# A fused attention and token-mixing MLP kernel: uneven filler batches, one paired maximum per stretch, and bursts cut in two in the MLP1 stage

## The chip, the cores and the metric

The kernel runs on one core of a Trainium2 chip. The metric is the device time of one execution in microseconds (us), the median of several runs. The time of a run is slightly longer than the span of its profile, which goes from the first to the last instruction.

## What is computed

```python
x = A_x                                             # (1, 2048, 640)
g = sigmoid((x * gate_w).sum(-1, keepdims=True))
# a: attention, 32 query heads of 20, one shared key/value head
q = (x @ wq).reshape(B, S, H, Dh).transpose(0, 2, 1, 3)
scores = einsum("bhqd,bkd->bhqk", q, x @ wk) * (Dh ** -0.5)
o = einsum("bhqk,bkd->bhqd", softmax(scores, axis=-1), x @ wv)
a = o.transpose(0, 2, 1, 3).reshape(B, S, H * Dh) @ wo
# b: MLP over the token axis
h = layernorm(x)                                    # (B, S, D)
u = gelu(einsum("bsd,sf->bdf", h, w1) + b1)         # F = 1728
b = (einsum("bdf,fs->bds", u, w2) + b2).transpose(0, 2, 1)
return g * a + (1 - g) * b
```

S is 2048, D is 640, F is 1728. The softmax subtracts a row maximum, so every score is computed twice: once as a "max tile" (queries on the partitions, reduced over 512 keys by VectorE) and once as a "score tile" (keys on the partitions, 512 queries, to which ScalarE applies the exponential).

## The kernel before

**Stages.** A prologue (projections, layer norm, the first ten tiles of the first MLP product) ends near 186 us. Then 248 **stretches** follow, counted by `j` in the loop `for j in range(n_st)`. Each holds 8 score tiles (`qk`, L689), some max tiles (`ms_next`, L507), some **fillers** (matmuls of 320 columns of the MLP or of the output projection), and ends in a **burst** (`burst`, L725): the products of exponentials and values for two key blocks, four heads side by side on the columns of the array. Stretches 0 to 71 take their fillers from the first MLP product (`b1_jobs`, L1020): this is the **MLP1 stage**. The next 128 take them from the second product (`b2_jobs`, L845), the last 48 from the output projection (`a_jobs`, L973).

**Two lanes.** Score tiles, max tiles and fillers contract over at most 64 rows, so two of them run at a time, one on each row half of the array. In stretch `j` the lane `h = j % 2` is the **own lane**: it holds the 8 score tiles and `own` max tiles. The **filler lane** holds the fillers and the remaining max tiles. A burst uses the whole array, so it begins only behind the last tile of both lanes.

**MLP1 before.** One tile of the first product is 96 steps, 48 for each lane. `batches` cuts them into two batches of 24, and each batch makes two stretches, one for each lane. A stretch holds 10 max tiles: `share` gives 8 to the own lane and 2 to the filler lane. The filler lane runs one max tile, 24 fillers and one max tile; the own lane runs `ssmSSmmssmssmmmm`, where `SS` is a pair of score tiles in neighbouring banks that one exponential of 1024 columns reads.

**Banks.** Seven PSUM banks rotate among score tiles, max tiles and the burst's sum (`xs3` has 3 neighbouring banks, `xs4` has 4); an eighth accumulates the fillers. A bank is taken again when ScalarE or VectorE has read it. The evicting copy of a burst (L749) is in ScalarE's queue, its addition to the running sum (L752) in GpSimd's.

**What sets the order.** A planner (`begins`, `issue`, `arrange`) keeps estimated clocks for the lanes, the banks, VectorE and ScalarE, and at each step issues the tile that can begin first. `begins` lets a filler start when its lane is free, and a tile that needs a bank only when its estimate says that one is free. The outcome is one fixed list of instructions for each engine. On the chip, semaphores decide when an instruction begins, but its place in the list is fixed.

**Weights.** The first product's weights arrive in chunks of 12 steps (`w1_upto`): GpSimd casts a chunk (L126) and subtracts (L127) for its low part. In this stage four chunk buffers serve, one of which is lent to queries, and the place of each conversion follows from the first and last use of its chunk.

Of the kernel before, what the change touches and what calls it, by code (L numbers as in the profile page):

```python
# [19 lines left out]
S, D, H, DH, F = 2048, 640, 32, 20, 1728  # L20
# [5 lines left out]
NB = 512  # L26
# [13 lines left out]
def mix_kernel(ctx: ExitStack, tc: tile.TileContext, A_x, A_wq, A_wk, A_wv, A_wo,  # L40
               B_x, B_w1, B_b1, B_w2, B_b2, gate_w, out):
    nc = tc.nc
    x = A_x[0]
# [440 lines left out]
    def span(i, n):  # L484
        t, at = (xs[0], i) if i < 3 else (xs[1], i - 3)
        return t[:, at * NB:(at + n) * NB]

    row_max, stores = {}, []
    mtiles = {}
# [3 lines left out]
    def ms_next(b):  # L493
        k = given[b]
        if k >= 32 * NU or k // 32 not in qtiles:
            return None
        given[b] += 1
        n, r = divmod(k, 32)
        (kq, pr), qt = divmod(r // 4, 2), r % 4

        def step(i=None):
            if n not in mtiles:
                mtiles[n] = mpool.tile([P, 16, 4], F32, name="mp")
            if i is None:
                turns[0] += 1
            ms = pre[turns[0] % 4].tile([P, NB], F32, name="x" if turns[0] % 4 else "g") if i is None else bank(i)
            mm = nc.tensor.matmul(ms, qtiles[n][64 * b:64 * b + 60, pr, qt * P:(qt + 1) * P],  # L507
                                  kst[64 * b:64 * b + 60, kq * NB:(kq + 1) * NB], start=True, stop=True)
            region = [("x", i)] if i is not None else []
            if region:  # L510
                touch(mm, writes=region)
            out = mtiles[n][:, (2 * b + pr) * 4 + qt, kq:kq + 1]

            def reduce():
                red = nc.vector.tensor_reduce(out, ms, axis=AX.X, op=ALU.max)  # L515
                if region:
                    touch(red, reads=region)
                issued[b] += 1

            return reduce  # L520

        return step

    def ms_done():
# [501 lines left out]
        return load, [([[of_chunk(base + st // HS, lambda h=h, st=st, k=k: mm(st, k, h)) for h in range(2)]  # L1026
                        for st in range(NS) for k in range(3)], done)]

    def batches(tiles, counts):
        out = []  # L1030
        for n, (load, parts, *_) in enumerate(tiles):
            for d, (steps, done) in enumerate(parts):
                cnt = counts.pop(0)
                rows = [[f[h] for f in steps if len(f) > h] for h in range(2)]
                cut = [[len(r) * j // cnt for j in range(cnt + 1)] for r in rows]
                for j in range(cnt):
                    rest = []
                    if d == 0 and j == 0 and n + 1 < len(tiles):
                        rest.append(tiles[n + 1][0])
                    out.append(([r[c[j]:c[j + 1]] for r, c in zip(rows, cut)], rest, [done] if j == cnt - 1 else []))  # L1040
        return out

    n_st = (len(units) - TAIL) // 2
    todo = [divmod(i, FC) for i in range(PRO, 2 * FC)]
    seq = batches([b1_jobs(*t) for t in todo], [2] * len(todo))
    m = len(seq)
    seq += batches([b2_jobs(st) for st in range(NS)], [2] * 2 * NS)
    seq[-1][1].append(second)
# [17 lines left out]
    step = 0  # L1066
# [13 lines left out]
    X_US, F_US, O_US = 0.2345, 0.1468, 0.869  # L1080
    W_US, FIRST_US, LAST_US, NEXT_US, SEEN_US = 0.11, 0.1, 0.333, 0.13, 0.43
    EACH = {"dve": (0.6, 0.84), "act": (0.48, 0.815)}
    PAIR_US = 0.85
    clock = {"dve": 0.0, "act": 0.0}
    lane, fresh, free = [0.0, 0.0], [True, True], [0.0] * 3 + [1.3] * 4
    state = {"at": 0.0, "f": 0.0, "last": 0.0}
# [2 lines left out]
    def spend(e, us, at=0.0):  # L1089
        clock[e] = max(clock[e], at) + us  # L1090
        return clock[e]
# [8 lines left out]

    def begins(h, kind):
        at = max(lane[h] + W_US * fresh[h], state["at"])
        if kind == "S":
            return max(at, pair[1] if pair else free[next_pair()])
        return max(at, state["f"] if kind in "fe" else min(free))

    def issue(h, kind, f):
        at = state["at"] = begins(h, kind)
        fresh[h] = False
        lane[h] = at + (F_US if kind in "fae" else X_US)  # L1110
        state["last"] = at
        if kind in "fae":
            f()
        elif kind == "S":
            if not pair:
                i = next_pair()
                pair[:] = [i, free[i + 1]]
                free[i] = free[i + 1] = float("inf")
            else:
                i = pair[0] + 1  # L1120
                begin = spend("act", PAIR_US, at + SEEN_US) - PAIR_US
                free[i - 1] = free[i] = begin + PAIR_US + EACH["act"][1] - EACH["act"][0]
                pair.clear()
            while any(k == i for _, k, _ in reduces):
                reduces.pop(0)[2]()
            f(i)
        else:
            i = next_free()
            each, hold = EACH["act" if kind == "s" else "dve"]
            begin = spend("act" if kind == "s" else "dve", each, at + SEEN_US) - each  # L1130
            free[i] = begin + hold
            while any(k == i for _, k, _ in reduces):
                reduces.pop(0)[2]()
            g = f(i)
            if kind == "m":
                reduces.append((begin, i, g))

    pairs = {}

    def layout(n_s, n_m, n_f, n_o):  # L1140
        if n_f > 22 and n_o > 1:
            places = [0, n_f]
        elif n_f > 22:
            places = [0]
        elif n_s + n_m < 13:
            places = [0, n_f - 4]
        else:
            places = [0, n_f]
        places = (places + [n_f // 2, 3 * n_f // 4])[:n_o]
        lf = ""  # L1150
        for i in range(n_f + 1):
            lf += "m" * places.count(i) + "f" * (i < n_f)
        lf += "m" * (n_o - lf.count("m"))
        if n_f > 22 and (n_s, n_m, n_o) == (8, 8, 2):
            return "ssmSSmmssmssmmmm", lf
        lx = "sSS" if n_s + n_m > 12 else "s"
        s, m = n_s - len(lx), n_m
        a, b = s, m
        while s or m:
            if m and (not s or m * a >= s * b):  # L1160
                lx, m = lx + "m", m - 1
            else:
                lx, s = lx + "s", s - 1
        return lx, lf

    def arrange(h, ss, own, other, fs, end):
        ss, own, other, fs = list(ss), list(own), list(other), list(fs)
        n_s, n_m, n_f = len(ss), len(own), len(fs)
        lx, lf = layout(n_s, n_m, n_f, len(other))
        pairs.clear()  # L1170
        at = lx.replace("m", "").find("S")
        if at >= 0:
            pairs.update({at: 0, at + 1: 2})
        lx = [(k, (own if k == "m" else ss).pop(0)) for k in lx]
        lf = [(k, (other if k == "m" else fs).pop(0)) for k in lf]
        lanes = [None, None]
        lanes[h], lanes[1 - h] = lx, lf
# [66 lines left out]
    def share(j):  # L1244
        h, to = j % 2, owed + wants[j]
        own = round((min(to, 9) + F_US / X_US * len(ph[j][0]) - 8) / 2)
        if h:
            own = (given[0] - given[1] + to + 1) // 2
        own = min(to, max(0, own))
        return (to - own, own) if h else (own, to - own)  # L1250

    for j in range(n_st):
# [36 lines left out]
        if j == 8 * 25 - 1:  # L1289
            new_q(29)  # L1290
        if j:
            burst((2 * j - 2, 2 * j - 1), (0, NB // 2, NB) if 15 < len(ph[j][0]) <= 22 else (0, NB))
        if j == n_st - 2:
            raw = last_wo()

# [185 lines left out]
```

## Time and profile before

| | before |
|---|---|
| median of 3 runs | 1597.38 us (1596.97 to 1598.45) |
| the profiled execution | 1597.11 us |
| its span | 1595.3 us |
| busy: PE, VectorE, ScalarE, GpSimd | 100%, 86%, 81%, 53% of the span |
| granted TensorE clock | 0.999 |
| MLP1 stretches | from 186.8 us (first burst) to 610.8 us (last) |

Instructions are named by line and operand tiles: L507 is a max tile's matmul, L515 its reduction, L689 a score tile, L701 its exponential, L1020 a filler of the MLP1 stage, L725 a burst. PE busy is a modelled share: matmuls overlap, so 100% says only that some matmul was always under way. What a stretch costs is read from the starts of the bursts, and from the pace at which each lane's matmuls begin.

### The profile page before, as it was taken

The page shows a single profiled execution, that of the slowest core. Times are in us where ns is not written, and L with a number is a line of the kernel's source. Part 1 is how long each engine was busy: PE and PEld are TensorE (multiplying, and loading weights), DVE is VectorE, ACT ScalarE, POOL GpSimd, SP SyncE. Part 2 cuts the span into 40 slices and gives each one's busy share as a digit, 9 for nine tenths or more (in the row PEclk, how much of TensorE's full clock was granted, in tenths as well). Part 3 has the DMA queues.
Part 4 walks back from the last instruction along what each step waited for, and adds up shares of the span by engine and source line. Part 5 has one row for each costly group of instructions (what it writes and reads, how often), then busy time and mean ns, then how long its engine had stood idle before and what let it go on. Part 6 is the DMA issues. An engine that isn't in the chain of part 4 may idle for free.

```text
span 1595.3 us, 43453 instructions
## 1 busy us (share of the span) xinstructions
PE 1589.4 (100%) x16907; PEld 1184.3 (74%) x16907; DVE 1379.2 (86%) x2626; ACT 1295.4 (81%) x2481; POOL 845.0 (53%) x930
## 2 busy tenths in 40 slices
PE   9999999999999999999999999999999999999998
PEld 7899876767677677777777777777777776666665
DVE  6689999999999999999999999999999996667743
ACT  4445677778787788888888888888888889999996
POOL 6567767777777777545554344444444433333340
PEclk9999999999999999999999999999999999999999
DMA  7665323222222232322121122122221113322341
GB/s 218 204 172 141 95 61 71 66 75 73 73 69 68 57 76 55 91 70 70 49 63 55 48 62 58 55 61 62 62 61 48 49 41 107 113 84 83 90 137 59
DMA packets 180452, 129.78 MB, mean 81 GB/s; under 512 B 41617, under 2 KB 150062, under 8 KB 180246
## 3 DMA queue, kind: packets, MB, share of 16 engines
q1 hardware_dynamic: 179958, 126.68, 28.6%
q8 instruction: 133, 2.18, 0.6%
q14 instruction: 73, 0.60, 0.1%
q10 hardware_dynamic: 288, 0.33, 0.1%
HBM read 93.57 MB, written 32.15 MB: 79 GB/s over the span
## 4 chain that ended last, share of the span: by engine, by line
PE 98%; SPq 1%; DVE 0%; ACT 0%; DMA 0%; issue 0%; DVEq 0%
PE xs L725 30%; PE xs L689 18%; PE xs L507 18%; PE g L845 11%; PE g L1020 7%; PE pu L634 4%; PE pp L303 4%; PE g L973 3%; PE x L507 1%; PE xs L927 1%; PE pt L295 0%; SPq L200 0%; DVE st L236 0%; PE xs L1426 0%; PE g L927 0%; PE xs L1446 0%
## 5 line engine op out<-in xcount | busy, mean ns | idle before, releaser
L515 DVE TENSOR_REDUCE mp<-xs 128x1 f32<-128x512 f32 x1946 | 1197.1, 682 | 133.0 <-PE xs L689 79.3
L701 ACT ACTIVATE p<-xs 128x512 f32<-128x512 f32 (+1 forms) x1841 | 1016.2, 677 | 7.4 <-PE xs L689 3.4
L752 POOL TENSOR_TENSOR osum<-osum,part 128x512 f32<-128x512 f32 x216 | 279.4, 1294 | 596.8 <-ACT part L749 574.8
L725 PE MATMUL xs<-p,v_sb 128*32 128x256 f32 (+1 forms) x6144 | 493.6, 454 | 0.0
L689 PE MATMUL xs<-q,kst 62*128 62x512 f32 x1344 | 476.9, 418 | 0.0
L507 PE MATMUL xs<-kst,q 60*128 60x512 f32 x1242 | 426.6, 407 | 0.0
L725 PEld LDWEIGHTS xs<-p,v_sb 128*32 128x32 f32 x6144 | 173.6, 109 | 210.7 <-issue 81.4
L689 PEld LDWEIGHTS xs<-q,kst 62*128 62x128 f32 x1344 | 236.8, 185 | 56.7 <-DVE mp L515 22.6
L749 ACT ACTIVATE part<-xs 128x256 f32<-128x256 f32 (+1 forms) x328 | 148.8, 454 | 157.1 <-PE xs L725 155.7
L1020 PE MATMUL g<-slot,w 64*128 64x320 f32 x1728 | 266.2, 305 | 0.0
L1020 PEld LDWEIGHTS g<-slot,w 64*128 64x128 f32 x1728 | 259.0, 184 | 1.8
L507 PEld LDWEIGHTS xs<-kst,q 60*128 60x128 f32 x1242 | 212.0, 184 | 50.3 <-DVE mp L515 19.3
L127 POOL TENSOR_TENSOR w<-wr,w 128x512 fp32r<-128x512 f32 (+1 forms) x180 | 225.0, 1252 | 35.1 <-ACT w L124 22.6
L689 PE MATMUL xs<-slot,kst 62*128 62x512 f32 x569 | 207.5, 418 | 0.0
L845 PE MATMUL g<-u,w 64*128 64x320 f32 x1296 | 200.4, 305 | 0.0
L845 PE MATMUL g<-slot,w 64*128 64x320 f32 x1296 | 200.4, 305 | 0.0
L507 PE MATMUL xs<-kst,slot 60*128 60x512 f32 x576 | 200.3, 408 | 0.0
L845 PEld LDWEIGHTS g<-u,w 64*128 64x128 f32 x1296 | 195.2, 184 | 1.6
L845 PEld LDWEIGHTS g<-slot,w 64*128 64x128 f32 x1296 | 195.2, 184 | 1.6
L973 PE MATMUL g<-slot 64*128 64x320 f32 x720 | 118.2, 306 | 0.0
L689 PEld LDWEIGHTS xs<-slot,kst 62*128 62x128 f32 x569 | 100.3, 185 | 20.1 <-ACT part L749 7.4
L973 PEld LDWEIGHTS g<-slot 64*128 64x128 f32 x720 | 111.8, 185 | 4.3 <-DVE mm L537 0.8
(190 smaller groups left out, 1435.7 us busy)
## 6 DMA issues: line engine op xcount, KB each, us to landing
wr<-in_B_w_dram SPq DMA_DIRECT2D x155, 256.0 KB
q<-q_scr SPq DMA_DIRECT2D x126, 80.0 KB
rb<-r_scr SPq DMA_DIRECT2D x120, 64.0 KB
slot<-o_scr SPq DMA_DIRECT2D x24, 320.0 KB
y_scr<-yo SPq DMA_DIRECT2D x16, 320.0 KB
q_scr<-qh SPq DMA_DIRECT2D x19, 256.0 KB
q_scr<-ql SPq DMA_DIRECT2D x19, 256.0 KB
o_scr<-rb SPq DMA_DIRECT2D x120, 40.0 KB
```

The costliest lines, as they stand in the source:

```text
L127: nc.gpsimd.tensor_sub(wl, wr, f32(wh))
L303: nc.tensor.matmul(pp, w, t, start=first and n == 0, stop=not more and n == len(steps) - 1)
L507: mm = nc.tensor.matmul(ms, qtiles[n][64 * b:64 * b + 60, pr, qt * P:(qt + 1) * P], kst[64 * b:64 * b + 60, kq * NB:(kq + 1) * NB], start= ...
L515: red = nc.vector.tensor_reduce(out, ms, axis=AX.X, op=ALU.max)
L689: mm = nc.tensor.matmul(s, kst[64 * b:64 * b + 62, kb * P:(kb + 1) * P], q[64 * b:64 * b + 62, pr, :], start=True, stop=True)
L701: act = nc.scalar.activation(p_all[:, a * NB:(j + 1) * NB], s, AF.Exp, scale=SCALE)
L725: mm = nc.tensor.matmul(o[32 * hh:32 * hh + 32, at:to], v_sb[:, units[u][1], :], p_all[:, j * NB + at:j * NB + to], start=first, stop=last ...
L749: touch(nc.scalar.activation(t[:, at:to], o[:, at:to], AF.Copy), [("x", i)])
L752: nc.gpsimd.tensor_add(osum[n], osum[n], t)
L845: other_tile(half, nc.tensor.matmul(hold["p"][:, :HD2], w[r, fc % HS, :], u[d][r, fc, :], start=(hold["n"] == 1), stop=(hold["n"] == 6 * F ...
L973: other_tile(half, nc.tensor.matmul(hold["p"][:, :HD2], o[r, c, :], w[r, c, d * HD2:(d + 1) * HD2], start=(hold["n"] == 1), stop=(hold["n" ...
L1020: other_tile(half, nc.tensor.matmul(hold["p"][:, :HD2], w[r, st % HS, :], h[d][r, st, :], start=(hold["n"] == 1), stop=(hold["n"] == 6 * NS)))
```

## The change

Four things change, all of them in the MLP1 stage:

- `batches` gets `more=1` there: the 48 steps of a lane are cut into 25 and 23. Two stretches of 25 and two of 23 alternate.
- A stretch of 25 has 9 max tiles in its own lane and 1 in the filler lane; a stretch of 23 has 8 and 2, as before. There are still 10.
- Two of the own lane's max tiles form a pair `M`, in neighbouring banks, and one reduction of 1024 columns gives both maxima. The own lane's order is a new string. Where two maxima would not lie side by side in the result tile (`turns`), the pair changes places with a single max tile. The paired exponential `SS` is gone from this stage.
- `burst` is cut into two halves of the queries, each with its own bank and its own eviction, as it already is in the stretches with 20 or 21 fillers.

```diff
...
-        def step(i=None):
+        def step(i=None, part=0):
...
-            out = mtiles[n][:, (2 * b + pr) * 4 + qt, kq:kq + 1]
+            col = (2 * b + pr) * 4 + qt
+            if part == 1:
+                return None
+            both = part == 2
+            out = mtiles[n][:, col - both:col + 1, kq]
+            if both:
+                ms = span(i - 1, 2).rearrange("p (a k) -> p a k", a=2)
+                region.append(("x", i - 1))
...
-                issued[b] += 1
+                issued[b] += 1 + both
...
+        step.turns = r % 8 == 7
...
-    def batches(tiles, counts):
+    def batches(tiles, counts, more=0):
...
-                cut = [[len(r) * j // cnt for j in range(cnt + 1)] for r in rows]
+                cut = [[len(r) * j // cnt + more * (0 < j < cnt) for j in range(cnt + 1)] for r in rows]
...
-    seq = batches([b1_jobs(*t) for t in todo], [2] * len(todo))
+    seq = batches([b1_jobs(*t) for t in todo], [2] * len(todo), 1)
...
-    PAIR_US = 0.85
+    PAIR_US = {"act": 0.85, "dve": 1.13}
...
-        if kind == "S":
+        if kind in "SM":
...
-        elif kind == "S":
+        elif kind in "SM":
+            e = "act" if kind == "S" else "dve"
...
-                begin = spend("act", PAIR_US, at + SEEN_US) - PAIR_US
-                free[i - 1] = free[i] = begin + PAIR_US + EACH["act"][1] - EACH["act"][0]
-                pair.clear()
+                begin = spend(e, PAIR_US[e], at + SEEN_US) - PAIR_US[e]
+                free[i - 1] = free[i] = begin + PAIR_US[e] + EACH[e][1] - EACH[e][0]
+                pair.append(begin)
...
-            f(i)
+            if kind == "S":
+                f(i)
+            else:
+                g = f(i, len(pair) - 1)
+                if g:
+                    reduces.extend(((begin, i - 1, g), (begin, i, lambda: None)))
+            if len(pair) > 2:
+                pair.clear()
...
-    def layout(n_s, n_m, n_f, n_o):
+    def layout(n_s, own, n_f, n_o):
+        n_m = len(own)
...
-        if n_f > 22 and (n_s, n_m, n_o) == (8, 8, 2):
-            return "ssmSSmmssmssmmmm", lf
+        if n_f > 22 and (n_s, n_m, n_o) == (8, 10 - n_o, n_o):
+            lx = list("smssmssmsmsmsMmm" if n_o == 1 else "smsmsssmmssmmsM")
+            at = lx.index("M")
+            if own[lx[:at].count("m")].turns:
+                to = at + 1 if "m" in lx[at:] else max(i for i in range(at) if lx[i] == "m")
+                lx[at], lx[to] = lx[to], lx[at]
+            return "".join(lx).replace("M", "MM"), lf
...
-        n_s, n_m, n_f = len(ss), len(own), len(fs)
-        lx, lf = layout(n_s, n_m, n_f, len(other))
+        n_f = len(fs)
+        lx, lf = layout(len(ss), own, n_f, len(other))
...
-        at = lx.replace("m", "").find("S")
+        at = lx.replace("m", "").replace("M", "").find("S")
...
-        lx = [(k, (own if k == "m" else ss).pop(0)) for k in lx]
+        lx = [(k, (own if k in "mM" else ss).pop(0)) for k in lx]
...
+        if len(ph[j][0]) > 22 and to == 10:
+            own = 8 + (len(ph[j][0]) > 24)
...
-            burst((2 * j - 2, 2 * j - 1), (0, NB // 2, NB) if 15 < len(ph[j][0]) <= 22 else (0, NB))
+            burst((2 * j - 2, 2 * j - 1), (0, NB // 2, NB) if len(ph[j][0]) > 15 else (0, NB))
...
```

Program order is shown below at three places. `xs_2756` is the tile of 3 banks, `xs_2760` that of 4; `g` is the fillers' bank; `kst` are keys, `q` and `slot_79` queries, `p` exponentials, `w_90` and `w_92` weight chunks. L507, L515, L689, L725 and L1020 are L507, L522, L697, L733 and L1028 in the changed kernel.

TensorE before, the end of the stretch whose burst is the 29th of the program; the last row is that burst:

```order
L1020 MATMUL g<-slot_80,w_90 128x320
L689 MATMUL xs_2760<-q,kst 128x512
L1020 MATMUL g<-slot_80,w_90 128x320 x2
L507 MATMUL xs_2760<-kst,slot_79 128x512
L1020 MATMUL g<-slot_80,w_90 128x320 x2
L507 MATMUL xs_2760<-kst,slot_79 128x512
L1020 MATMUL g<-slot_80,w_90 128x320
L507 MATMUL xs_2760<-kst,slot_79 128x512
L1020 MATMUL g<-slot_80,w_90 128x320 x2
L507 MATMUL xs_2756<-kst,slot_79 128x512 x2
L725 MATMUL xs_2756<-p,v_sb 32x512 x8
```

Of 70 MLP1 stretches behind the first burst, 68 end like this: the filler lane's last max tile is the only tile, with one of the own lane, behind all 24 fillers.

TensorE in the changed kernel, the end of the same stretch, which now has 25 fillers:

```order
L507 MATMUL xs_2760<-kst,slot_79 128x512
L1028 MATMUL g<-slot_80,w_90 128x320 x2
L697 MATMUL xs_2756<-q,kst 128x512
L1028 MATMUL g<-slot_80,w_90 128x320 x2
L507 MATMUL xs_2756<-kst,slot_79 128x512
L1028 MATMUL g<-slot_80,w_90 128x320 x4
L507 MATMUL xs_2756<-kst,slot_79 128x512
L1028 MATMUL g<-slot_80,w_92 128x320
L507 MATMUL xs_2760<-kst,slot_79 128x512 x2
L733 MATMUL xs_2760<-p,v_sb 32x256 x16
```

The pair is the two tiles of `xs_2756` around the four fillers. 24 of the 25 fillers now stand ahead of the pair's second tile, and two more own tiles follow it. Of the 34 stretches with 25 fillers, 22 have three own tiles behind the 24th filler as here, 9 have two, and 3 have four.

TensorE in the changed kernel, the end of the next stretch, which has 23 fillers:

```order
L1028 MATMUL g<-slot_80,w_90 128x320 x2
L507 MATMUL xs_2760<-kst,slot_79 128x512
L1028 MATMUL g<-slot_80,w_90 128x320 x2
L697 MATMUL xs_2756<-q,kst 128x512
L1028 MATMUL g<-slot_80,w_90 128x320 x3
L507 MATMUL xs_2756<-kst,slot_79 128x512
L507 MATMUL xs_2760<-kst,slot_79 128x512 x2
L733 MATMUL xs_2756<-p,v_sb 32x256 x8
L733 MATMUL xs_2760<-p,v_sb 32x256 x8
```

Here the filler lane's last max tile (`xs_2756`) and then both tiles of the pair (`xs_2760`) stand behind all 23 fillers. 17 of the 36 stretches with 23 fillers end with three max tiles behind the last filler; 12 end with one or two tiles behind the fillers, as before; in 7 the pair stands earlier and a score tile and a max tile follow it behind the fillers.

VectorE in the changed kernel, early in the stage, from one row that marks the end of a stretch's fillers (`flag`) to the next:

```order
L719 MEMSET flag 1x1
L522 TENSOR_REDUCE mp<-xs_2760 128x2
L522 TENSOR_REDUCE mp<-xs_2756 128x1
L522 TENSOR_REDUCE mp<-xs_2760 128x1
L522 TENSOR_REDUCE mp<-xs_2756 128x1
L522 TENSOR_REDUCE mp<-xs_2760 128x1
L522 TENSOR_REDUCE mp<-xs_2756 128x1 x2
L522 TENSOR_REDUCE mp<-xs_2760 128x1
L522 TENSOR_REDUCE mp<-xs_2756 128x1
L719 MEMSET flag 1x1
L522 TENSOR_REDUCE mp<-xs_2756 128x1
```

Eight single reductions and one over two banks (`128x2`) stand where ten single ones stood.

## The prediction, made before the run

> **What bounds the kernel now.** I read the windows first, for who is busy in the stage that changes, then the order of time within a stretch, for what each lane does there.
>
> ```profile
> core 0: us, PE busy (x) PEld busy (x) DVE busy (x) ACT busy (x) POOL busy (x), PEclk, DMA share, GB/s
> 424.00:520.00 96.00, 96.00 (x928) 68.32 (x924) 95.98 (x182) 75.42 (x139) 69.87 (x84) 1.00 0.26 67
> 620.00:720.00 100.00, 100.00 (x1242) 77.94 (x1240) 91.38 (x172) 87.93 (x169) 53.43 (x64) 1.00 0.26 71
> ```
>
> In the MLP1 stage (first window) VectorE (DVE) is busy 95.98 of 96 us, and so is PE, though PE's share is modelled. ScalarE and GpSimd have a fifth to a quarter of their time to spare. Two engines may set the pace there. The timeline of PE gives the length of a stretch, and its rows inside one stretch say of what it is made.
>
> ```profile
> 186.78 1.92 PE L725 MATMUL xs<-p,v_sb 128*32 128x512 f32 x16
> ...
> 404.82 1.92 PE L725 MATMUL xs<-p,v_sb 128*32 128x512 f32 x16
> 406.67 0.50 PE L689 MATMUL xs<-w,kst 62*128 62x512 f32 x1
> 407.01 0.45 PE L1020 MATMUL g<-slot,w 64*128 64x320 f32 x2
> ...
> 410.41 0.30 PE L1020 MATMUL g<-slot,w 64*128 64x320 f32 x1
> 410.51 0.42 PE L507 MATMUL xs<-kst,q 60*128 60x512 f32 x2
> 410.89 1.92 PE L725 MATMUL xs<-p,v_sb 128*32 128x512 f32 x16
> ...
> 610.79 1.92 PE L725 MATMUL xs<-p,v_sb 128*32 128x512 f32 x16
> ```
>
> From the first MLP1 burst to the last, 70 stretches take 610.79 - 186.78 = 424.0 us, **6.06 us each**. In the stretch shown, the burst holds the array for 406.67 - 404.82 = 1.85 us. The lanes' second tiles begin 0.34 us behind the first. The 24 fillers begin from 407.01 to 410.41, 23 gaps of 3.40 / 23 = 0.148 us: the filler lane never pauses. The own lane's pace is plainest in the last stage, where it is the longer lane, and the prologue shows a stream that is alone on the array:
>
> ```profile
> 1503.01 0.39 PE L689 MATMUL xs<-q,kst 62*128 62x512 f32 x1
> 1503.24 0.39 PE L689 MATMUL xs<-q,kst 62*128 62x512 f32 x1
> ...
> 1504.18 0.39 PE L689 MATMUL xs<-q,kst 62*128 62x512 f32 x1
> ...
> 1505.09 0.39 PE L689 MATMUL xs<-q,kst 62*128 62x512 f32 x1
> 1505.41 0.64 PE L725 MATMUL xs<-p,v_sb 128*32 128x512 f32 x4
> ...
> 23.47 3.48 PE pp L303 x15
> ```
>
> A tile of 512 columns takes 0.235 us (five gaps in 1504.18 - 1503.01); 3.48 / 15 = 0.232 us alone, so an idle neighbour lane hardly helps. A burst begins 1505.41 - 1505.09 = 0.32 us behind the start of the last tile.
>
> The filler lane's sum is then 0.34 + 24 x 0.148 = 3.89 us to the start of its last max tile, + 0.32 to the burst, + 1.85 = **6.06**, the measured length. VectorE's own sum comes close:
>
> ```profile
> 430.22 1.28 DVE L515 TENSOR_REDUCE mp<-xs 128x1 f32<-128x512 f32 x2
> 431.42 0.21 DVE L537 TENSOR_REDUCE mm<-mp 128x16 f32<-128x64 f32 x1
> 431.54 4.88 DVE L515 TENSOR_REDUCE mp<-xs 128x1 f32<-128x512 f32 x8
> ...
> 436.34 6.07 DVE L515 TENSOR_REDUCE mp<-xs 128x1 f32<-128x512 f32 x10
> ...
> 442.33 1.27 DVE L515 TENSOR_REDUCE mp<-xs 128x1 f32<-128x512 f32 x2
> ```
>
> Ten reductions take 442.33 - 436.34 = 5.99 us, 0.599 each, and small operations like L537 take some 0.12 us in about every second stretch, 5.99 + 0.06 = 6.05. So PE's filler lane and VectorE are balanced to within 0.01 us, and only a change that shortens both shortens the stage.
>
> **The change part by part.** *Paired maximum.* Not in this trace. A 64-column reduction holds VectorE for 431.54 - 431.42 = 0.12 us and a 512-column one 0.599: (0.599 - 0.12) / 448 = 1.07 ns a column, so 1024 columns take 0.599 + 512 x 0.00107 = 1.15. The ends are one single reduction, 0.60, and two, 1.20, or 1.36 by two whole durations (6.07 - 9 x 0.599 = 0.68 each). I take 1.15. VectorE's sum falls from 6.05 to 6.00, at worst rises to 6.21.
>
> *Fillers of 25 and 23, and the order.* This is the large term, and it is PE's. Matmuls begin in program order, so a lane's tile begins no earlier than the fillers listed ahead of it. Without a pause, 25 fillers and 17 own tiles would give 0.34 + 15 x 0.235 = 3.87 to the last own tile, and 23 fillers 3.74 to the filler lane's last max tile; with 0.32 and the burst of 1.86 (below) 6.05 and 5.92, a mean 0.07 shorter than now. The order has pauses, though: before, one tile of the own lane stands behind all fillers; now up to four of its 0.235 us tiles stand behind the 24th, while the filler lane has nothing left. The 24th filler begins at 0.34 + 23 x 0.148 = 3.74. With n own tiles behind it the last begins at 3.74 + (n - 1) x 0.235, and the stretch lasts 2.18 more:
> - 25 fillers: n = 3 in 22 stretches, 6.39 (+0.33); n = 2 in 9, 6.16 (+0.10); n = 4 in 3, 6.63 (+0.57). Sum 7.3 + 0.9 + 1.7 = +9.9 us.
> - 23 fillers: the filler lane's last max tile begins at 3.74. In 12 stretches it is the last: 5.92 (-0.14), -1.7 us. In 17 the pair stands behind the last filler too; its second tile begins 0.235 later: 6.16 (+0.10), +1.7. In 7 a score and a max tile follow, +0.10 in four, and +0.33 in the three where a pair tile does too: +1.4. Sum +1.4 us.
>
> Together **+11.3 us**. The first two stretches get one filler more each, 2 x 0.148 = +0.3.
>
> The Trainium skill, "TensorE: Matmul & The Clock Gate", Part 3 ("The mechanism"), says that matmuls are strictly first in, first out, and that only weight loads are pulled ahead. By that the pauses stay on the chip even where a bank is free early, and the sum is the one above; if matmuls could pass each other it would be the pause-free -0.07 x 70 = -5 us. The rows above do begin in program order, but none has a tile ready behind one that waits.
>
> *Bursts in halves.* The next stage has them already:
>
> ```profile
> 627.30 1.93 PE L725 MATMUL xs<-p,v_sb 128*32 128x256 f32 x32
> 629.16 0.49 PE L507 MATMUL xs<-kst,q 60*128 60x512 f32 x1
> ...
> L749 ACT ACTIVATE part<-xs 128x256 f32<-128x256 f32 x214 | 82.1, 383 | 67.1 <-PE xs L725 66.9
> L701 ACT ACTIVATE p<-xs 128x1024 f32<-128x1024 f32 x59 | 61.8, 1048 | 0.0
> L749 ACT ACTIVATE part<-xs 128x512 f32<-128x512 f32 x52 | 31.1, 598 | 64.7 <-PE xs L725 64.7
> ```
>
> 629.16 - 627.30 = 1.86 us, 0.01 more, already in the sum. On ScalarE two evictions of 383 ns replace one of 598, and the first lies in time in which ScalarE waited for the burst (64.7 us over 52 bursts, 1.2 each). That wait also hides the lost paired exponential, under 0.2 us by 1048 against two singles. If the cover were gone, the exponentials would come up to 0.2 us later; they feed the next burst, and their banks feed the own lane. I cost both at nothing. GpSimd still adds once per burst.
>
> *Weights.* The 25th step belongs to the third chunk, so GpSimd now converts two chunks in a row between two MLP tiles:
>
> ```profile
> 416.78 0.61 POOL L126 CAST w<-wr 128x512 fp32r<-128x512 f32 x1
> 417.47 1.28 POOL L127 TENSOR_TENSOR w<-wr,w 128x512 fp32r<-128x512 f32 x1
> 419.68 1.30 POOL L752 TENSOR_TENSOR osum<-osum,part 128x512 f32<-128x512 f32 x1 [0.93 <-ACT part L749]
> ```
>
> One takes about 2.0 us; a second behind it would end near 420.7. That chunk is first used by the 25th filler of a stretch that begins near 418.9, at 418.9 + 0.34 + 24 x 0.148 = 422.8. Two us to spare; the burst's addition and the gelu steps behind it move by as much, into idle time. Were the cover gone, 2 us in each of 18 tiles. The weights' DMAs come as often as before. I take nothing.
>
> *Waits for banks.* The pair needs two neighbours. How long is not in this trace. The nearest row is an exponential's hold, about 0.5 us a tile (3.96 us for eight):
>
> ```profile
> 407.36 3.96 ACT L701 ACTIVATE p<-xs 128x512 f32<-128x512 f32 x7
> ```
>
> From nothing, if the pauses in the order cover it, to 0.5 in each of the 25 stretches with n of 3 or 4. I take nothing, since the pause of two or three fillers is that long already, and keep +6 us, half of it, for the range. Below nothing: fillers run at 2.64 us for 36 in two lanes in the prologue, 0.147, so some 0.03 us of each present stretch may be waits for VectorE, which would now have more time: up to -2 us.
>
> ```profile
> 175.99 2.64 PE pu L634 x36
> ```
>
> **Sum.** 11.3 + 0.3, less half of those 2 us: +10.6 on the profiled execution's 1597.11 gives 1607.7. The median of the runs lies 0.3 above that execution: **1608.0 us**.
>
> **The rivals.** *VectorE decides, and the stage gets faster.* VectorE is the engine without idle time, and one instruction fewer saves 0.05 us a stretch: 70 x 0.05 = -3.6, 1593.8 us. It wins if PE's pauses cost nothing, that is, if own tiles really begin at 0.235 us throughout. For it: 95.98 of 96 us busy. Against it: the filler lane accounts for 6.06 us alone, and the order puts tiles behind fillers that cannot begin earlier. 9%. The Trainium skill, "VectorE: DVE Perf Modes", "Rules for kernel authors", speaks for this rival: it wants the number of operations small, since each is flushed from the pipeline by itself. The slope above agrees that 0.05 us per reduction is fixed cost.
>
> *The tail is cheap, and nothing changes.* If own tiles behind the last filler began at half their spacing, 0.117, the pauses would lose about 10 us of their cost and the time would be near 1598. It decides from a spacing under 0.15. The lone stream at 0.232 speaks against it. 5%.
>
> *Bank waits come on top*, as bounded above: 1614 or more, 8%. A paired maximum that costs 1.36 us would change nothing: VectorE at 6.21 would be no later than PE's mean of 6.06 + 11.3 / 70 = 6.22.
>
> **How the numbers follow.** The forecast has 78%, mostly 1604 to 1611. With half of the bank waits above it and a part of the cheap tail below, 1602.5 to 1614 leaves out about 18%. Slower by over 0.2% (3.2 us, about what a measurement can tell): 86%; within it 5%; faster 9%.
>
> **What would show it.** Bursts 6.4 us apart in most stretches with 25 fillers, and 5.9 or 6.16 with 23; VectorE idle some 0.2 us a stretch, waiting for PE; 1.15 us for the paired maximum. Wrong would be a stage in which bursts stay at or under 6.0 us, or pairs that begin before the fillers ahead of them.

## The result and the profile after

| | before | after |
|---|---|---|
| median of the runs | 1597.4 us | 1617.62 us (1617.06 to 1617.75, 4 runs) |
| ratio to before, 95% interval | | 1.0125 [1.0112, 1.0137] |
| span of the profiled execution | 1595.3 us | 1615.9 us |
| MLP1 stretches, mean of 70 | 6.06 us | 6.34 us |

The kernel became slower by 20.2 us, not by the predicted 10.6. All of it lies in the MLP1 stage. The timeline of PE after (start, duration, engine, line and operation) has these first and last MLP1 bursts:

```profile
187.71 0.85 PE L733 MATMUL xs<-p,v_sb 128*32 128x256 f32 x12
...
631.59 1.72 PE L733 MATMUL xs<-p,v_sb 128*32 128x256 f32 x28
```

631.59 - 187.71 = 443.9 us against 424.0 before: +19.9. The first burst comes 187.71 - 186.78 = 0.93 later. Together 20.8, which the difference of the spans, 20.6, agrees with. The window that was shown of before, of the changed kernel:

```profile
core 0: us, PE busy (x) PEld busy (x) DVE busy (x) ACT busy (x) POOL busy (x), PEclk, DMA share, GB/s
424.00:520.00 96.00, 96.00 (x1133) 75.12 (x1127) 92.56 (x159) 78.32 (x166) 67.31 (x79) 1.00 0.25 66
```

VectorE fell from 95.98 to 92.56 of 96 us: 3.44 / 96 x 6.34 = 0.23 us idle in each stretch. It no longer sets the pace. PE still shows 96.00, which says nothing, as before. The groups of VectorE in the stage (duration in ns behind the bar, then idle time and what ended it) show why the one term about VectorE held:

```profile
L522 DVE TENSOR_REDUCE mp<-xs 128x1 f32<-128x512 f32 x563 | 347.5, 682 | 18.1 <-PE xs L507 8.6 <-PE xs L697 8.5
L522 DVE TENSOR_REDUCE mp<-xs 128x2 f32<-128x1024 f32 x69 | 84.2, 1220 | 0.3
```

A pair takes 1220 ns where a single takes 682; each overlaps the next by 0.08 us (0.68 less the slot of 0.599), so its slot is 1.14 us, against 1.15 predicted.

Where the 19.9 us came from is seen when the 70 stretches are sorted by the end of their program order, as the prediction did. The periods are differences of burst starts in the timeline; the last columns are the mean time between the start of the last filler and the burst, and the sum of the gaps between fillers beyond 0.148 us.

| stretches | predicted | measured | last filler to burst | pauses of fillers |
|---|---|---|---|---|
| before, 70 of 24 fillers | | 6.06 | 0.47 | 0.02 |
| 22 of 25, three own tiles behind the 24th filler | 6.39 | 6.42 | 0.69 | 0.01 |
| 9 of 25, two | 6.16 | 6.18 | 0.44 | 0.01 |
| 3 of 25, four | 6.63 | 6.62 | 0.90 | 0.00 |
| 12 of 23, one tile last | 5.92 | 6.02 | 0.59 | 0.00 |
| 17 of 23, three max tiles last | 6.16 | 6.52 (6.19 to 6.83) | 1.08 | 0.00 |
| 4 of 23, score and max tile last | 6.16 | 6.20 | 0.75 | 0.02 |
| 3 of 23, pair tile with them | 6.39 | 6.43 | 0.99 | 0.00 |

The filler lane runs without a pause in every class; what is lost lies behind the last filler, where the own lane still has tiles to begin. With 25 fillers the sizes agree with the prediction within 0.03 us. The 17 stretches of 23 miss by 0.36 each, 6.1 us, the 12 by 0.10. The end of one of the 17, on PE and on VectorE:

```profile
267.49 0.60 PE L1028 MATMUL g<-slot,w 64*128 64x320 f32 x3
267.93 0.40 PE L507 MATMUL xs<-kst,q 60*128 60x512 f32 x1
268.52 0.73 PE L507 MATMUL xs<-kst,q 60*128 60x512 f32 x2 [0.19 <-DVE flag L719]
269.18 1.93 PE L733 MATMUL xs<-p,v_sb 128*32 128x256 f32 x32
```

```profile
267.18 1.89 DVE L522 TENSOR_REDUCE mp<-xs 128x1 f32<-128x512 f32 x3
268.40 0.06 DVE L719 MEMSET flag<- 1x1 f32 x1
```

The filler lane's max tile follows the last filler at 267.93, and then nothing begins for 0.59 us. The second of the three reductions ends at 267.18 + 0.60 + 0.68 = 268.46, and the pair's first tile begins at 268.52, 0.06 behind it: it waited for the bank that this reduction read. The view names the flag, a row of 0.06 us that ended at the same moment. Such a wait can't be seen in the order, because no filler is left to stand ahead of it. Each engine's instruction list names the semaphore signal that a tile waits for, and the trace has its time: in 12 of the 17 a tile behind the last filler begins within 0.06 us of the signal that frees its bank, in 5 VectorE's and in 7 ScalarE's. These 12 take 6.42 to 6.83 us; the other five take 6.19 to 6.20, close to the predicted 6.16.

So there were two theories to tell apart. **Order theory**, the prediction's: tiles can't begin before the fillers listed ahead of them, and that costs. **Bank theory**: tiles wait for banks that VectorE or ScalarE still reads, both where the order shows pauses and where it shows none.

### The profile page after: what moved, and what is told of

It reads as the page before. It is cut to its first block, busy times and chain, and to the rows that moved or that the text cites. A ratio compares the mean times of both kernels' runs of the same rounds, so it can differ in the third digit from the quotient of the medians.

```text
span 1615.9 us, 45794 instructions
## 1 busy us (share of the span) xinstructions
PE 1609.0 (100%) x18043; PEld 1229.8 (76%) x18043; DVE 1381.6 (85%) x2556; ACT 1320.9 (82%) x2622; POOL 846.0 (52%) x930
## 4 chain that ended last, share of the span: by engine, by line
PE 96%; DVE 2%; SPq 1%; ACT 1%; issue 0%; DMA 0%; DVEq 0%
PE xs L733 29%; PE xs L507 18%; PE xs L697 18%; PE g L853 10%; PE g L1028 6%; PE pu L642 4%; PE pp L303 4%; PE g L981 3%; DVE mp L522 1%; PE x L507 1%; PE xs L935 1%; ACT p L709 1%; PE pt L295 0%; SPq L200 0%; DVE st L236 0%
## 5 line engine op out<-in xcount | busy, mean ns | idle before, releaser
L522 DVE TENSOR_REDUCE mp<-xs 128x1 f32<-128x512 f32 (+1 forms) x1876 | 1198.1, 704 | 150.2 <-PE xs L697 78.4
L733 PE MATMUL xs<-p,v_sb 128*32 128x256 f32 (+1 forms) x7280 | 494.3, 409 | 0.0
L697 PE MATMUL xs<-q,kst 62*128 62x512 f32 x1344 | 484.8, 414 | 0.0
L507 PE MATMUL xs<-kst,q 60*128 60x512 f32 x1242 | 442.4, 412 | 0.7 <-DVE flag L719 0.7
L733 PEld LDWEIGHTS xs<-p,v_sb 128*32 128x32 f32 x7280 | 210.5, 109 | 209.3 <-ACT p L709 54.2
L757 ACT ACTIVATE part<-xs 128x256 f32<-128x256 f32 (+1 forms) x390 | 159.5, 409 | 148.2 <-PE xs L733 146.5
L697 PEld LDWEIGHTS xs<-q,kst 62*128 62x128 f32 x1344 | 243.4, 185 | 46.1 <-ACT part L757 19.8
L1028 PE MATMUL g<-slot,w 64*128 64x320 f32 x1728 | 265.6, 305 | 0.0
L1028 PEld LDWEIGHTS g<-slot,w 64*128 64x128 f32 x1728 | 259.0, 184 | 1.6
L507 PEld LDWEIGHTS xs<-kst,q 60*128 60x128 f32 x1242 | 210.0, 184 | 44.3 <-ACT part L757 25.1
L697 PE MATMUL xs<-slot,kst 62*128 62x512 f32 x569 | 208.8, 416 | 0.0
L507 PE MATMUL xs<-kst,slot 60*128 60x512 f32 x576 | 205.2, 411 | 0.3 <-DVE flag L719 0.2
L697 PEld LDWEIGHTS xs<-slot,kst 62*128 62x128 f32 x569 | 101.2, 185 | 18.2 <-ACT part L757 8.6
```

Of the source, the lines that this page charges most:

```text
L697: mm = nc.tensor.matmul(s, kst[64 * b:64 * b + 62, kb * P:(kb + 1) * P], q[64 * b:64 * b + 62, pr, :], start=True, stop=True)
L733: mm = nc.tensor.matmul(o[32 * hh:32 * hh + 32, at:to], v_sb[:, units[u][1], :], p_all[:, j * NB + at:j * NB + to], start=first, stop=last ...
L757: touch(nc.scalar.activation(t[:, at:to], o[:, at:to], AF.Copy), [("x", i)])
L1028: other_tile(half, nc.tensor.matmul(hold["p"][:, :HD2], w[r, st % HS, :], h[d][r, st, :], start=(hold["n"] == 1), stop=(hold["n"] == 6 * NS)))
```

## The experiments

All ratios are to runs of the kernel before on the same chip, three rounds each.

**One part taken out of the changed kernel, at a time.** First the pair as two single tiles:

```diff
-            return "".join(lx).replace("M", "MM"), lf
+            return "".join(lx).replace("M", "mm"), lf
```

> The changed kernel with the two tiles of the pair turned into two single max tiles (two banks, two reductions of 512 columns); batches of 25 and 23 and halved bursts stay. Order theory (only the pauses that stand in the program order cost): by the prediction's own sums the 34 stretches of 25 fillers take about 6.14 us (their last own tile stands one place nearer to the 24th filler), the 36 of 23 take 5.92, a mean of 6.03, so 1595 to 1597 us. Bank theory (the pair holds two neighbouring banks for one long reduction, and its tiles wait for them behind the last filler, where the order can't show it): the waits of 0.3 to 0.6 us that 17 stretches showed behind the last filler are gone, no stretch of 23 is over 6.3; 0.1 us a stretch stays, in which the halved burst waits for its first bank: 1597 to 1601 us. Both put nearly all of the loss on the pair; if the time stays over 1607, the pair isn't the cause and both fall.

1600.55 us, ratio 1.0019 [1.0009, 1.0029]. Bank theory's range holds it: all 36 stretches of 23 fillers take 6.0 us, none is over 6.07, and those of 25 take 6.19 on average. 17 of the 20 us hang on the pair, together with its order: the planner puts single tiles in other places, so this run changes both.

Next, whole bursts again, with the batches and the pair kept:

```diff
-            burst((2 * j - 2, 2 * j - 1), (0, NB // 2, NB) if len(ph[j][0]) > 15 else (0, NB))
+            burst((2 * j - 2, 2 * j - 1), (0, NB // 2, NB) if 15 < len(ph[j][0]) <= 22 else (0, NB))
```

> The changed kernel with bursts of 512 columns in one bank in the MLP1 stage, as before the change; uneven batches and the pair stay. The order changes with it: more own tiles stand behind the last filler (five of them with 25 fillers in some 17 stretches), 0.12 us a stretch by the prediction's sums. Order theory: 1617.6 + 70 x 0.12 = 1626 us. Bank theory: a burst that takes one bank rather than two leaves one more to the pair, so that the waits behind the last filler shrink and part of the 8 us comes back: 1616 to 1622 us.

1627.55 us, ratio 1.0189 [1.0172, 1.0206], 1.5 us over order theory's number and well over bank theory's range. The bank that a whole burst leaves free did not help; 17 stretches of 25 now end with three max tiles behind the last filler and take 6.66. The time speaks for sums over the order, and against what bank theory was made to say. The waits themselves are there all the same: in each of these 17 an own tile begins within 0.06 us of the signal that VectorE has read its bank, and the three tiles follow behind it. So the tails of this order are waits on the chip too, and one bank less for the burst did not shorten them.

Then batches of 24 and 24, with the pair and the halved bursts kept:

```diff
-    seq = batches([b1_jobs(*t) for t in todo], [2] * len(todo), 1)
+    seq = batches([b1_jobs(*t) for t in todo], [2] * len(todo))
```

> The changed kernel with batches of 24 and 24 rather than 25 and 23; pair and halved bursts stay. By the prediction's sums over the order it is 0.09 us a stretch above the kernel before: order theory 1597.4 + 6 = 1603 to 1605 us. Bank theory: some 27 of 70 stretches end in three max tiles behind four fillers, with the pair among them, and wait there as 17 stretches of the changed kernel did, 0.2 to 0.6 us each: 1609 to 1616 us.

1613.52 us, ratio 1.0101 [1.0086, 1.0116], as bank theory has it. The 27 stretches with three max tiles last take 6.15 to 6.83, where the order alone asks for 6.15.

**The pauses taken out of the order.** This is the direct test of the prediction's largest term.

```diff
-        if kind in "SM":
+        if kind == "M":
+            return at
+        if kind == "S":
             return max(at, pair[1] if pair else free[next_pair()])
```

> The changed kernel, except that the program order puts the pair's tiles as early as their lane is free, without leaving fillers ahead of them while their banks are still read: the sum over the order alone is 0.07 us a stretch under the kernel before (no pauses). Order theory: the pauses were the cost, so 1592 to 1596 us. Bank theory: the pair's tiles now wait at the head of TensorE's list for their two banks and hold up the fillers behind them, so nothing is won: 1612 us or more, and stretches in which a filler waits behind a tile of the pair.

1619.18 us, ratio 1.0135 [1.012, 1.015]. Order theory falls: without the listed pauses the stretches still take 6.36 us on average, 26 of those with 25 fillers 6.51. The end of one of them on PE, and VectorE at that time:

```profile
365.18 0.50 PE L507 MATMUL xs<-kst,slot 60*128 60x512 f32 x1
365.28 0.32 PE L1028 MATMUL g<-slot,w 64*128 64x320 f32 x1
365.68 0.50 PE L507 MATMUL xs<-kst,slot 60*128 60x512 f32 x1
365.68 0.56 PE L1028 MATMUL g<-slot,w 64*128 64x320 f32 x2
```

```profile
364.94 1.28 DVE L522 TENSOR_REDUCE mp<-xs 128x1 f32<-128x512 f32 x2
```

The first reduction ends at 364.94 + 0.68 = 365.62, and the tile begins at 365.68, the same 0.06 behind. Now the tile stands early in the list, and the fillers behind it wait with it: 365.68 - 365.28 = 0.40 us instead of 0.148. In those 26 stretches the fillers pause for 0.44 us a stretch, where they paused for 0.01 in the changed kernel. The wait was only moved.

**The readers cut short.** If tiles wait for a bank to be read, a shorter read must give the time back, in an unchanged order. First VectorE's, in the changed kernel:

```diff
+            ms = ms[:, :cut[0]]
...
-                ms = span(i - 1, 2).rearrange("p (a k) -> p a k", a=2)
+                ms = span(i - 1, 2).rearrange("p (a k) -> p a k", a=2)[:, :, :cut[0]]
...
+        cut[0] = NB // 2 if len(ph[j][0]) > 22 else NB
```

> The changed kernel in the same order on every engine, but the maxima of the MLP1 stage read 256 of their 512 columns (512 of 1024 in the pair): half the keys are left out of the maximum, so each reduction gives its bank back earlier and VectorE has time to spare. Bank theory (the pair's tiles wait behind the last filler for banks that a reduction still reads): the 17 stretches of 23 fillers that end in three max tiles, 6.52 us on average, fall to the 6.19 of the quickest of them; the stretches of 25 keep their 6.2 to 6.6, because their pauses are written in the order, and the twelve at 6.02 stay, because ScalarE frees their bank: 1617.6 - 17 x 0.33 = 1612, 1610 to 1613 us. Order theory (the missing time has to do with the order or with a fixed price of tiles behind the last filler, not with how long a reduction reads): unchanged within 2 us, 1615.5 to 1619.5.

1610.37 us, ratio 1.0081 [1.0066, 1.0096]. The total is in bank theory's range, but that is luck: it came from another place than I wrote. The 17 stretches fell only to 6.39; the 22 stretches of 25, which were to keep the pauses of the order, fell from 6.42 to 6.23. The list of each engine tells which semaphore the tile behind the four fillers waits for: VectorE's in 14 of the 22, ScalarE's in 8. All 14 fell, to between 6.04 and 6.18; all 8 stayed at 6.38 to 6.43. The same stretch in the changed kernel and here:

```profile
331.53 0.45 PE L1028 MATMUL g<-slot,w 64*128 64x320 f32 x2
331.70 0.45 PE L507 MATMUL xs<-kst,q 60*128 60x512 f32 x1
331.82 0.60 PE L1028 MATMUL g<-slot,w 64*128 64x320 f32 x3
332.24 0.49 PE L507 MATMUL xs<-kst,q 60*128 60x512 f32 x1
332.26 0.45 PE L1028 MATMUL g<-slot,w 64*128 64x320 f32 x2
332.58 0.62 PE L507 MATMUL xs<-kst,q 60*128 60x512 f32 x2
333.13 0.42 PE L733 MATMUL xs<-p,v_sb 128*32 128x256 f32 x4
```

```profile
329.59 0.40 PE L508 MATMUL xs<-kst,q 60*128 60x512 f32 x1
329.71 0.30 PE L1030 MATMUL g<-slot,w 64*128 64x320 f32 x1
329.82 0.39 PE L508 MATMUL xs<-kst,q 60*128 60x512 f32 x1
329.86 0.45 PE L1030 MATMUL g<-slot,w 64*128 64x320 f32 x2
330.06 0.39 PE L508 MATMUL xs<-kst,q 60*128 60x512 f32 x1
330.15 0.30 PE L1030 MATMUL g<-slot,w 64*128 64x320 f32 x1
330.29 0.39 PE L508 MATMUL xs<-kst,q 60*128 60x512 f32 x1
330.30 0.30 PE L1030 MATMUL g<-slot,w 64*128 64x320 f32 x1
330.61 0.42 PE L735 MATMUL xs<-p,v_sb 128*32 128x256 f32 x4
```

The program order of both ends like this (line numbers left out):

```
MATMUL xs_2760<-kst,q 128x512
MATMUL g<-slot_80,w_91 128x320 x4
MATMUL xs_2760<-kst,q 128x512
MATMUL g<-slot_80,w_92 128x320
MATMUL xs_2756<-kst,q 128x512
MATMUL xs_2760<-kst,q 128x512
```

In the first stretch the pair's second tile begins at 332.24. VectorE's second reduction in the row below ends at 330.91 + 0.60 + 0.68 = 332.19.

```profile
330.91 1.88 DVE L522 TENSOR_REDUCE mp<-xs 128x1 f32<-128x512 f32 x3
```

In the second stretch nothing waits, and the order is not kept: of the four fillers listed between the tiles at 329.59 and 329.82 only one begins between them, and the last two tiles begin ahead of a filler that is listed before both. The own lane simply goes on at its 0.235 us. So this place behind four fillers in the list costs nothing by itself.

The same cut in the order without pauses:

> The order without planned pauses (the pair's tiles as early as their lane is free), with the maxima of the MLP1 stage read over 256 of 512 columns. In that order with whole maxima, 26 stretches of 25 fillers took 6.51 us on average although they have few tiles behind the last filler. Bank theory: those were waits at the head of TensorE's list for banks that VectorE still reads; with half the reading they are gone, stretches of 25 take 6.05 to 6.19 and those of 23 take 6.02: a mean of 6.03 to 6.1, 1596 to 1601 us. If it isn't the time that a bank is read (two neighbours at once, or the burst's two banks, whoever reads them): 6.3 us a stretch, 1612 us or more.

1606.82 us, ratio 1.006 [1.0045, 1.0075], between the two expectations: 12.4 us came back, and stretches of up to 6.88 stayed. What stayed is ScalarE's: of the 62 tiles in this run that begin within 0.06 us of the signal for their bank, 61 wait for an exponential and one for a reduction; with whole maxima it was 62 and 49. The view of waits shows only those before which the array was idle, 3.1 us in 12 waits:

```profile
PE xs L508 <- ACT p L711: 3.1, 12, 0.5
```

The same cut in the kernel before, as a control:

> Control: the kernel before in the same order on every engine, with the maxima of the MLP1 stage read over 256 of 512 columns. If TensorE's filler lane alone sets 6.06 us a stretch, as the prediction has it, nothing changes: 1596 to 1598 us. If VectorE's sum of 6.05 us also sets the pace, some stretches fall under 6.03 and the time falls by up to 2 us: 1595 to 1596.

1596.79 us, ratio 0.9996 [0.9986, 1.0005]: no difference. Before the change, the filler lane set the 6.06 us, though VectorE was busy all the time.

**Both readers cut short.** ScalarE's exponentials too, in the listed order and in the order without pauses (the cut of the maxima as above):

```diff
-            act = nc.scalar.activation(p_all[:, a * NB:(j + 1) * NB], s, AF.Exp, scale=SCALE)
+            e = (j + 1) * NB - (short[0] if n_exp == 1 else 0)
+            act = nc.scalar.activation(p_all[:, a * NB:e], s[:, :e - a * NB], AF.Exp, scale=SCALE)
...
+        short[0] = NB // 2 if len(ph[j][0]) > 22 and j > 9 else 0
```

> The changed kernel in the same order on TensorE, but both readers of the rotating banks are cut short in the MLP1 stage: the maxima read 256 of 512 columns (512 of 1024 in the pair), and from the tenth stretch on each exponential covers 256 of 512 queries, so half of the exponentials are left out there. Bank theory (each pause is a tile's wait for a bank that VectorE or ScalarE still reads, and a place behind a filler in the list costs nothing of itself): the prediction's pause-free sums come true, 6.05 us with 25 fillers and 5.92 with 23, a mean of 5.98: 1591 to 1597 us. Order theory (a tile can't begin before the fillers listed ahead of it): not under the 1606 to 1608 us that the prediction worked out from the order. If ScalarE's hold doesn't matter, it stays at the 1610 us of the run with short maxima alone.

> The order without planned pauses, with both readers cut short as in the run before this one (maxima over 256 of 512 columns, half of the exponentials left out from the tenth stretch on). Bank theory: the two orders differ only in where a tile waits, so without waits they take the same time, within 2 us of the run before this one: 1591 to 1597 us. If waits in the middle of a stretch come from something other than these readers (the burst's evictions, the weight loads), stretches over 6.3 us stay, 1600 us or more.

1595.16 us, ratio 0.9987 [0.9978, 0.9996], and 1593.45 us, ratio 0.9974 [0.9965, 0.9983]. Bank theory's numbers come true in both. In the listed order the 22 stretches of 25 take 6.07 on average, the 12 of 23 take 5.92, and the 17 take 6.00 instead of 6.52. Four bursts in a row of that run, around two of the 17 and one of the 22:

```profile
308.61 1.93 PE L736 MATMUL xs<-p,v_sb 128*32 128x256 f32 x32
314.50 1.93 PE L736 MATMUL xs<-p,v_sb 128*32 128x256 f32 x32
320.39 1.93 PE L736 MATMUL xs<-p,v_sb 128*32 128x256 f32 x32
326.44 0.85 PE L736 MATMUL xs<-p,v_sb 128*32 128x256 f32 x12
```

5.89, 5.89 and 6.05 us are the sums without any pause, 5.92 and 6.05, which the prediction worked out first and then left. The order is still that of the changed kernel, with every pause listed. These kernels leave work out and are no candidates; they show what the waits cost: 1617.6 - 1595.2 = 22.4 us, of which 7.2 came with the maxima and 15.2 more with the exponentials. Tiles that begin within 0.06 us of the signal for their bank, in the same order of all engines and the same 70 stretches: 76 in the changed kernel (49 for ScalarE, 27 for VectorE), 61 with the maxima cut (all for ScalarE), 8 with both cut. Each time the signal is that of the instruction that read the tile's own bank.

The exponentials were not cut in the kernel before, so that control is missing. A rival would be bursts that wait for the values of the exponentials. The lists exclude it for the start of the burst: in the changed kernel, wherever its first matmul waits for an exponential, this is one that read the burst's bank, never one whose result the burst uses.

**Each part alone, on the kernel before.** The pair (own lane `ssmSSmmssmssmmM`), the halved bursts (the last diff line on `burst`), and the batches (own lane `ssmSSmmssmssmmmmm` with 25 fillers):

> The kernel before with one edit: the last two max tiles of the own lane become a pair with one reduction of 1024 columns. Batches of 24, whole bursts and the paired exponential stay as before. By the prediction's sums over its order, 26 of 70 stretches end 0.09 us later (their pair's second tile behind the last filler), the others as before: order theory 1597.4 + 2.3 = 1599 to 1601 us. Bank theory: the pair waits for two neighbours in stretches of 24 too, 0.2 to 0.4 us in at least those 26: 1604 to 1612 us.

> The kernel before with one edit: the bursts of the MLP1 stage in two halves of the queries with two banks; batches of 24, no pair, the paired exponential stays. Its order puts three max tiles behind the last two or three fillers in 21 of 70 stretches, 0.15 us each by the prediction's sums. Order theory: 1597.4 + 3.3 = 1600 to 1601 us. Bank theory: with 24 fillers the burst's first bank is free in time (in stretches of 23 the burst came 0.1 us late for it), so at most a few tenths in those 21: 1597 to 1600 us.

> The kernel before with one edit: batches of 25 and 23 fillers rather than 24 and 24, with 9 and 1 or 8 and 2 max tiles in the lanes; no pair, whole bursts, the paired exponential stays. By the prediction's sums over its order 25 fillers cost 0.12 us more and 23 as much less. Order theory: 1596 to 1598 us. Bank theory: no more banks are taken than before, and ten single reductions still take VectorE 6.05 us a stretch, so no gain either: 1596 to 1599 us, with VectorE's wait carried from one stretch to the next. Over 1601 us the uneven batches would have a price of their own, which neither has.

| alone | time | ratio to before | over 1597.4 |
|---|---|---|---|
| pair | 1605.94 us | 1.0052 [1.0035, 1.0068] | +8.5 us |
| halved bursts | 1601.99 us | 1.0029 [1.0018, 1.004] | +4.6 us |
| batches of 25 and 23 | 1604.39 us | 1.0044 [1.0027, 1.0061] | +7.0 us |

The pair is where bank theory put it, with 28 stretches at 6.20 that the order leaves as they were; in each of them an own max tile begins within 0.06 us of the exponential that frees its bank. The other two cost more than either theory said. That the three add up to 20.1 is no proof that they don't interact: batches and halved bursts together, in the planner's order for single tiles, cost only 3.1 us (the first run). With halved bursts alone, 21 stretches end with three or four max tiles behind the last filler and take 6.23 us on average; in each of them a score tile waits for an exponential to free its bank, which happens in two of the other 49.

For the batches alone the trace shows the price. The 34 stretches of 25 take 6.23 and the 36 of 23 take 6.04, where the prediction's sums over this order are 3.74 + 0.235 + 0.32 + 1.85 = 6.15 and 0.235 less, 5.91. Against 6.06 before, that is 5.3 us over 70 stretches, and the first burst comes at 188.29, 1.5 us late. In 34 of the 36 stretches of 23 the burst begins within 0.06 us of the exponential that frees its bank. In a stretch of 25 the own lane, with 9 max tiles, has 17 tiles, 0.34 + 15 x 0.235 = 3.87 us to the last, and the filler lane 0.34 + 24 x 0.148 = 3.89: they are equally long, and the own lane's waits no longer lie beside fillers. That this is the reason is argued, not tested. Why the first burst is late stays open.

## Why the prediction was wrong

- **What bounds the kernel.** Right: the filler lane's 6.06, as the control shows. What it hid was not said: before, the own lane's 16 tiles end 0.34 + 14 x 0.235 + 0.32 + 1.85 = 5.80 us into a stretch, 0.26 before the filler lane, and waits of the own lane disappear in that. There are such waits: in each of the 70 stretches before, a score tile begins within 0.06 us of the reduction that frees its bank.
- **"Matmuls begin in program order, so a lane's tile begins no earlier than the fillers listed ahead of it."** This step is wrong. Tiles of the two row halves begin up to three places out of the listed order when none waits, and the same order takes 6.42 or 6.07 us in its 22 stretches of 25 fillers, depending on how long a bank is read. The +9.9 for 25 fillers came out (10.7 measured) because the order was planned around the same bank times, and the chip waits there too: in each of the 22 stretches with three own tiles behind the 24th filler, the first of these begins within 0.06 us of the signal for its bank. The place behind a filler is a copy of the wait, not its cause. The Trainium skill, "TensorE: Matmul & The Clock Gate", Part 3 ("The mechanism"), whose rule that matmuls start strictly in order the prediction weighed, does not agree with these rows: 24 of 70 stretches of the run with both readers cut short, in the listed order, have a tile three fillers ahead of its place, by up to 0.43 us. The few rows that the prediction showed begin in program order, but the whole trace before did not: in each of its 70 stretches some matmul begins ahead of one of the other row half that is listed before it, by at most 0.11 us.
- **"Waits for banks. ... I take nothing, since the pause of two or three fillers is that long already."** This is the step that failed in size. Waits for banks are the whole loss, as far as the short readers can show it: 22.4 us when they go. 6.1 us of what was missing are the 17 stretches of 23 fillers, where the order can show no wait; 1.2 are the 12 whose burst waits 0.10 us for a bank, in each case one that an exponential still reads. On the profiled execution 20.6 - 10.6 = 10.0 us were missing: 7.6 in the stretches of 23 fillers, 0.8 in those of 25, and 1.6 in the two terms of the next point. The upper end of 0.5 us in 25 stretches was set on the stretches with 25 fillers, not on those that needed it.
- **Deductions.** The -1 for VectorE's earlier freedom was nothing: the control gained 0.6 us, less than can be measured. The first two stretches cost 0.9, not 0.3; but the runs with the maxima cut and with both readers cut, which are alike up to there, have their first bursts at 187.23 and 186.69, so 0.6 us is not clear of their spread.
- **Paired maximum, halves, weights.** 1.14 us against 1.15; VectorE idle 0.23 against 0.2. "I cost both at nothing" for the bursts was wrong: alone they cost 4.6 us. That they take two banks is the likely reason, but no run separates it from the order that came with them. MLP2 and the last stage kept their 5.50 and 4.73 us a stretch.
- **Rivals.** VectorE as the bound fell: it became idler and the time grew. "Bank waits come on top", 8%, was the outcome in its time; but the waits are also what the pauses in the order stand for, and do not come on top of those.

That banks are short here agrees with the Trainium skill, "TensorEngine Tiling (Array Packing)", "Gotcha 1: PSUM Pressure", which warns that row tiles, each writing to another bank, press on PSUM; how much, only the runs above say.

## What to carry to other kernels

When a planner has put a pause into an instruction list, ask what the pause was put there for: the list shows the wait, not what ends it, and at the end of a stage, where nothing is left to list ahead, it shows nothing. A resource with no slack (here seven banks) is tested by shortening its readers in an unchanged order; taking the pauses out of the list only moves them. An engine that is busy all the time may still have its waits covered by another lane; count that cover before spending it on an even balance.

## What the runs showed of the hardware

- Matmuls on the two row halves begin out of the listed order, up to three places apart, in the run with both readers cut short. One that waits for a semaphore held back both halves in the order without pauses: 0.40 us between fillers instead of 0.148.
- A tile that follows a waiting tile on its row half begins 332.58 - 332.24 = 0.34 us behind it, not 0.235, and the waiting tile shows 0.49 us instead of 0.39. The other stretch shown gives the same, 268.52 + 0.73 - 0.40 = 268.85, 0.33 behind 268.52. In these two a wait cost about 0.1 us more than itself.
- A tile begins 0.05 to 0.06 us behind the end of the reduction that frees its bank (three cases above), and 0.043 us at the least behind the signal that it waits for (all tiles of the MLP1 stage in the changed kernel).
